# Branch hints ahead of the last branches of SyncE, VectorE and TensorE, with SyncE's end in a block of its own

## Chip, cores, metric

One Trainium2 chip, one core of it. The metric is the device time of one execution in microseconds (us); a time quoted for a kernel is the median of its runs on the chip.

## The reference

One decoding step for 8 sequences: attention of one query against a cache of 4096 keys and values in 32 heads of 128, beside a GELU MLP, added up.

```python
def _A_ref(x, k_cache, v_cache, wq, wo):        # B, H, Sk, Dh = 8, 32, 4096, 128
    q = (x @ wq).reshape(B, 1, H, Dh) ...
    p = softmax(einsum("bhqd,bhkd->bhqk", q, k_cache) * Dh ** -0.5)
    return einsum("bhqk,bhkd->bhqd", p, v_cache) ... @ wo
def _B_ref(x, w1, b1, w2, b2):
    return gelu(layernorm(x) @ w1 + b1) @ w2 + b2
xn = layernorm(x)
return x + _A_ref(xn, ...) + _B_ref(xn, ...)
```

Keys and values are 2 x 268 MB in bf16. Everything else is small beside them.

## The kernel before

SyncE issues all large loads in order: wq, w1, then K and V in 32 tiles (equal parts), then w2 and wo. Each load has 128 rows, in the trace 128 packets; a K or V load lands 19.35 us after the one before it and one of its 64 KB packets takes 2.42 us, so each of the 16 DMA engines has 8 of them. SyncE's queue keeps the 16 engines busy for 99.7% of the span. VectorE multiplies K by the query, TensorE sums and then weights V; a last block of PE multiplies by w2 and wo. In the profile VectorE is DVE, TensorE is PE (its weight loads PEld), ScalarE is ACT, and SPq is SyncE's sequencer, which issues loads. PE's program is 783 instructions long: a prologue, a loop over tiles, and the last block written out.

```python
    # SyncE: the K and V loads, then the last weights, then the end
    for t in range(1, NT):
        sy.wait_ge(sem["kf"], NX * (t - 1) + 2)
        load_kv(k_v, t, 0)
        sy.wait_ge(sem["vf"], t)
        load_kv(v_v, t, 1)
    # [cut: w2]
    for n, (r0, r1) in enumerate(zip(CUTS, CUTS[1:])):      # wo in four pieces
        if n == 1:
            sy.wait_ge(sem["kf"], NX * (NT - 1) + 5)
        wo_in.append(nc.alloc_semaphore(f"in_wo{n}"))
        sy.dma_start(out=wo_rows(r0, r1), in_=wo_v[:, r0 * D:r1 * D]).then_inc(wo_in[-1], 16)
    # [cut]
    sy.wait_ge(fin_d, 1)
    sy.dma_start(out=out2[:, :ND], in_=fin[:B]).then_inc(sem["out"], 16)
    sy.sem_inc(sent)
    sy.wait_ge(sem["out"], 32).then_inc(sem["out"], -32)

    # VectorE and ScalarE: a loop of 16 turns of two tiles, then the end
    with nc.Fori(0, NT // 2, 1, engines=[ENG.DVE, ENG.Activation]) as it:
        for u in range(2):
            vector_tile(2 * it + u, u)
            scalar_tile(u)
    # [cut]
    ve.wait_ge(sem["end"], 2)
    ve.tensor_copy(out=fin[:B], in_=acc[0][:B, :ND]).then_inc(fin_d, 1)

    # TensorE: blocks "head", "tile", "product", "values", "project"
    te.br_lt(regs["turns"], NT, on_true="tile", on_false="project")
    block("project")
    # [cut: 72 matmuls on w2, 8 on the heads]
    for n, (r0, r1) in enumerate(zip(CUTS, CUTS[1:])):
        te.wait_ge(wo_in[n], 16)
        rows = wo_rows(r0, r1).rearrange("p (r d) -> p r d", d=D)
        for r in range(r0, r1):
            ins = accumulate(te, OT[:, r, :], rows[:, r - r0, :], stop=(r == RO - 1))
    ins.then_inc(sem["end"], 1)
```

The softmax here doesn't subtract the row's maximum and nothing guards it: scores larger than these inputs give would overflow.

## Time and profile before

| | before |
|---|---|
| median of the first 3 runs | 1292.96 us |
| span of the profiled run | 1291.5 us |
| mean DMA rate | 431 GB/s |
| fetches of code in the span | 3 of 16 KB, 1 of 8 KB |

The page of the kernel before, its head, the DMA row of the 40 slices (busy tenths), and its table of DMA queues (packets, MB, share of the 16 engines):

```profile
span 1291.5 us, 14658 instructions
PE 736.8 (57%) x4707; PEld 322.3 (25%) x4707; DVE 829.4 (64%) x740; ACT 56.8 (4%) x181; POOL 2.4 (0%) x12
...
DMA  9999999999999999999999999999999999999998
...
q1 hardware_dynamic: 10368, 556.93, 99.7%
q8 instruction: 3, 0.05, 0.0%
q10 hardware_dynamic: 38, 0.02, 0.0%
q14 instruction: 1, 0.01, 0.0%
```

No engine is near full, the DMA is. The packets of the two queues of kind "instruction" are told here as the engines' code fetches: by their sizes 16 KB each on q8 (16,384 bytes), 8 KB each on q14 (8,192 bytes). That the large ones are TensorE's and the small ones VectorE's or SyncE's is read from their times.

The chain that ended last, in order of time (start, length, what):

```profile
1259.36 0.33 SPq L481
1259.69 0.05 issue
1259.74 28.52 DMA ring<-in_A_wo_dram
1288.26 0.04 issue
1288.31 1.29 PE acc L374 x18
1289.60 0.02 issue
1289.62 0.45 DVE fin L604
```

The end hangs on the landing of the third piece of wo at 1288.26 us. What comes after it takes 3.2 us.

The trace has 16 records of the load's semaphore, the counter that PE waits on, for each load, one for each DMA engine; PE's next matmul starts 0.05 us after the sixteenth (1288.31 after 1288.26 us). For that piece of wo, these are the times of the 16 records, against the last one:

```
before, third piece of wo (last at 1288.26 us):
-1.88 -1.88 -1.87 -1.80 -1.74 -1.63 -1.62 -1.58 -1.53 -1.46 -1.42 -1.41 -1.38 | -0.20 -0.11 0.00
```

Thirteen engines are done 1.4 us before the end, three are late. The three late ones go back to the fetches. The DMA table of the kernel before for 28 to 33, 50 to 55, 74 to 79 and 1286 to 1290 us, in this order:

```profile
q1 hardware_dynamic: 32, 2.10, 97.3%
q8 instruction: 1, 0.02, 1.3%
...
q1 hardware_dynamic: 31, 2.03, 94.6%
q14 instruction: 1, 0.01, 0.4%
...
q1 hardware_dynamic: 31, 2.03, 94.4%
q8 instruction: 1, 0.02, 1.3%
...
q1 hardware_dynamic: 170, 0.44, 27.5%
q8 instruction: 1, 0.02, 1.7%
```

The packets of the trace give their times, and, followed engine by engine (a data packet starts 3 or 4 ns before its forerunner ends), what each does to its engine:

| start | size | took | the engine's next 64 KB data packet (elsewhere 2.42 us) | lateness left behind |
|---|---|---|---|---|
| 29.93 us | 16 KB | 1.018 us | 2.886 us | 1.49 us |
| 52.15 us | 8 KB | 0.309 us | 3.033 us | 0.92 us |
| 75.96 us | 16 KB | 1.048 us | 2.888 us | 1.52 us |

(The last column is the fetch and what the next packet took over 2.418 us.) A further 16 KB at 1287.07 us falls on an engine that has just delivered its last data, and 8 KB at 1291.59 us come after the last wait of SyncE. The landings of the first loads show when an engine falls behind: one late engine at 46 us, two at 66 us, three at 85 us, and three ever after.

### The profile page before, as it was taken

The numbers are of one execution on the slowest core, as the hardware profiler recorded it, in microseconds if no ns is written. First come the engines' busy times: TensorE is split into PE (matmuls) and PEld (weight loads), VectorE is DVE, ScalarE is ACT, GpSimd is POOL, SyncE is SP. The second block draws the span as 40 slices with busy tenths as digits, with TensorE's granted clock in tenths as the row PEclk, the third lists the DMA queues.
The fourth block names the chain that finished last, engine by engine and source line by source line (L and its number), as shares of the span: only waits on it lengthen the run. The fifth ranks groups of instructions, "written<-read, shape, count | busy, mean of one in ns | idle before, by whom it ended". The sixth has DMA issues, their size and how long they took to land. (4 is left out here: it accounts for less than half of the span.)

```text
span 1291.5 us, 14658 instructions
## 1 busy us (share of the span) xinstructions
PE 736.8 (57%) x4707; PEld 322.3 (25%) x4707; DVE 829.4 (64%) x740; ACT 56.8 (4%) x181; POOL 2.4 (0%) x12
## 2 busy tenths in 40 slices
PE   4654565554565554665554565554566554565557
PEld 1222232222222222222222232222222222222223
DVE  2655677655677655677655677655677655577654
ACT  2000000000000000000000000000000000000000
POOL 0000000000000000000000000000000000000000
PEclk8778887778887777887777887778887777888779
DMA  9999999999999999999999999999999999999998
GB/s 419 441 427 440 430 428 449 422 428 449 422 428 449 422 430 447 422 436 440 424 436 438 426 438 434 428 442 428 428 449 422 428 449 422 428 449 422 430 447 350
DMA packets 10410, 557.02 MB, mean 431 GB/s; under 512 B 1163, under 2 KB 1188, under 8 KB 1446
## 3 DMA queue, kind: packets, MB, share of 16 engines
q1 hardware_dynamic: 10368, 556.93, 99.7%
q8 instruction: 3, 0.05, 0.0%
q10 hardware_dynamic: 38, 0.02, 0.0%
q14 instruction: 1, 0.01, 0.0%
HBM read 556.94 MB, written 0.01 MB: 431 GB/s over the span
## 5 line engine op out<-in xcount | busy, mean ns | idle before, releaser
L643 PE MATMUL s_ps<-ring,ident 128*128 x2048 | 544.5, 423 | 514.1 <-PEq L641 513.1
L559 DVE TENSOR_TENSOR ring<-ring,qb 128x4096 bf16<-128x4096 bf16 x256 | 579.2, 2283 | 281.6 <-DMA ring<-in_A_k_cache_dram 281.3
L643 PEld LDWEIGHTS s_ps<-ring,ident 128*128 128x128 bf16 x2048 | 217.4, 106 | 828.3 <-issue 678.5
L534 DVE TENSOR_REDUCE sc<-s_ps 128x32 f32<-128x512 f32 x256 | 171.8, 684 | 0.0
L662 PE MATMUL o_ps<-ring,ebd 128*32 128x512 bf16 x2048 | 116.4, 380 | 0.0
L546 DVE TENSOR_TENSOR ebd<-es,head 128x1536 bf16<-128x1536 bf16 x64 | 77.9, 1218 | 0.0
L569 DVE RECIPROCAL rec<-tot_ps 128x8 f32<-128x8 f32 x32 | 6.6, 208 | 110.7 <-PE oT_ps L670 110.7
L582 ACT ACTIVATE es<-sc 128x192 bf16<-128x192 f32 x64 | 19.8, 310 | 1104.2 <-DVE sc L534 1104.2
L662 PEld LDWEIGHTS o_ps<-ring,ebd 128*32 128x32 bf16 x2048 | 51.6, 97 | 62.5 <-issue 13.6
L670 PE MATMUL oT_ps<-selc,ob 128*128 128x8 f32 x256 | 33.9, 259 | 12.3 <-ACT ob L586 12.3
L670 PEld LDWEIGHTS oT_ps<-selc,ob 128*128 128x128 f32 x256 | 31.0, 191 | 15.2 <-ACT ob L586 15.2
L586 ACT ACTIVATE ob<-o_ps 128x512 f32<-128x512 f32 x32 | 19.1, 597 | 80.2 <-PE o_ps L662 80.2
L425 DVE TENSOR_SCALAR ring<-ring 96x384 f32<-96x384 f32 x2 | 0.7, 352 | 26.4 <-ACT ring L424 26.4
L545 DVE TENSOR_TENSOR Es<-Ep 128x1 f32<-128x1 f32 x32 | 5.1, 160 | 13.3 <-ACT es L582 13.3
L666 PEld LDWEIGHTS tot_ps<-headf,Es 128*128 128x128 f32 x64 | 9.5, 187 | 13.6 <-issue 13.6
L666 PE MATMUL tot_ps<-headf,Es 128*128 128x8 f32 x64 | 12.4, 266 | 0.0
L582 ACT ACTIVATION_READ_ACCUMULATOR es<-sc 128x1 f32 x64 | 11.9, 186 | 0.0
L414 PE MATMUL o_ps<-ring 128*32 128x384 bf16 x27 | 7.8, 860 | 2.8 <-DMA ring<-in_B_w_dram 2.8
L574 DVE TENSOR_TENSOR Ox<-on,quad 128x32 bf16 x32 | 6.2, 192 | 4.8
L414 PE MATMUL s_ps<-ring 128*32 128x384 bf16 x27 | 7.9, 862 | 0.0
L374 PE MATMUL acc<-ring,hT_sb 128*8 128x288 bf16 x72 | 6.0, 335 | 2.8 <-DMA ring<-in_B_w_dram 2.8
L336 PE MATMUL tot_ps<-ident,ring 40*128 40x16 bf16 x9 | 0.7, 204 | 11.8 <-DVE ring L314 11.8
(76 smaller groups left out, 61.2 us busy)
## 6 DMA issues: line engine op xcount, KB each, us to landing
ring<-in_B_w_dram SPq DMA_DIRECT2D x2, 5184.0 KB, 25.2
ring<-in_A_wq_dram SPq DMA_DIRECT2D x1, 4608.0 KB, 13.7
ring<-in_A_wo_dram SPq DMA_DIRECT2D x1, 1728.0 KB, 28.6
ring<-in_A_wo_dram SPq DMA_DIRECT2D x1, 1584.0 KB, 26.5
ring<-in_A_wo_dram SPq DMA_DIRECT2D x1, 1008.0 KB, 28.5
ring<-in_A_k_cache_dram SPq DMA_DIRECT2D x32, 31.9
ring<-in_A_v_cache_dram SPq DMA_DIRECT2D x32, 30.5
ring<-in_A_wo_dram SPq DMA_DIRECT2D x1, 288.0 KB, 28.8
```

Source lines behind the costliest of these rows:

```text
L414: i = e.matmul(h_ps[j][s * MP:(s + 1) * MP], lhsT=lhsT, rhs=wv[:, r0:r0 + HK, :], **flags)
L534: ins = ve.tensor_reduce(out=sc[:, n * CB:(n + 1) * CB], in_=bank_of(x).rearrange("p (c d) -> p c d", d=DL), axis=AX.X, op=ALU.add)
L546: ve.tensor_tensor(out=ebd[:, ja:jb], in0=es[:, a:b].rearrange("p (j c) -> p j c", c=4).unsqueeze(2) .to_broadcast([P, nj, G, 4]), in1=hea ...
L559: ve.tensor_tensor(out=k, in0=k, in1=qb[:, bass.ds(t, 1), :].to_broadcast([P, CB, Dh]), op=ALU.mult,).then_inc(sem["prod"], 1)
L569: ve.reciprocal(out=rec[:], in_=tot_ps[:, :G]).then_inc(sem["rec"], 1)
L574: ve.tensor_tensor(out=Ox[:, bass.ds(t, 1)].rearrange("p o g m -> p (o g) m"), in0=on[:].unsqueeze(2).to_broadcast([P, G, M]), in1=quad[:] ...
L582: sa.activation(out=es[:, a * CB:b * CB], in_=sc[:, a * CB:b * CB], func=ACT.Exp, scale=scale, accum_out=Ep[:, i:i + 1]).then_inc(sem["x"], 1)
L586: sa.activation(out=ob[:].rearrange("r c d -> r (c d)"), in_=o_ps, func=ACT.Copy).then_inc(sem["ob"], 1)
L643: ins = te.matmul(to, lhsT=idn, rhs=k[:, :, d * DL:(d + 1) * DL], start=(d == 0), stop=(d == Dh // DL - 1))
L662: ins = te.matmul(o_ps[m * MP:(m + 1) * MP, :], lhsT=ebd[:, j].rearrange("p g c -> p (g c)"), rhs=vals[:, c:c + 4, :], start=(j < M), stop ...
L666: te.matmul(tot_ps[:, :G], lhsT=Es[:].to_broadcast([P, P]), rhs=headf[:], start=True, stop=True).then_inc(sem["vf"], 1)
L670: ins = te.matmul(oT_ps[:, :G], lhsT=ob[:, c, :], rhs=selc[:, c, :], start=(c == 0), stop=(c == 3))
```

## The change

Its intent: to be rid of the fetches at 52.15, 1287.07 and 1291.59 us, which I took to bring code that their engine does not run; the trace does not show what a fetch brings. In the program a hint names the last branch and its target ahead of time; that the fetch is then not made was my hope. A hint is put on a branch, so SyncE's last four instructions go into a block of their own, and VectorE and TensorE get an empty last block.

```diff
+    vector_last = nc.mark_branch_hint_location(ENG.DVE)      # at the start of the program
+    sync_last = nc.mark_branch_hint_location(ENG.SP)
@@ SyncE, after the last piece of wo is issued
+    sy.br("sync_end").branch_hint(sync_last)
@@
-    sy.wait_ge(fin_d, 1)
-    sy.dma_start(out=out2[:, :ND], in_=fin[:B]).then_inc(sem["out"], 16)
-    sy.sem_inc(sent)
-    sy.wait_ge(sem["out"], 32).then_inc(sem["out"], -32)
@@ after the last work of VectorE
+    ve.br("vector_end").branch_hint(vector_last)
+    block("vector_end", ENG.DVE)
+
+    block("sync_end", ENG.SP)
+    sy.wait_ge(fin_d, 1)
+    sy.dma_start(out=out2[:, :ND], in_=fin[:B]).then_inc(sem["out"], 16)
+    sy.sem_inc(sent)
+    sy.wait_ge(sem["out"], 32).then_inc(sem["out"], -32)
@@ TensorE
     block("project")
+    place = nc.mark_branch_hint_location(ENG.PE)
@@
     ins.then_inc(sem["end"], 1)
+    te.br("tensor_end").branch_hint(place)
+    block("tensor_end")
```

More of the change, by code (lines that the diff above doesn't have):

```diff
@@ L480, in decode @@
         wo_in.append(nc.alloc_semaphore(f"in_wo{n}"))
-        sy.dma_start(out=wo_rows(r0, r1), in_=wo_v[:, r0 * D:r1 * D]).then_inc(wo_in[-1], 16)
+        to, rows = wo_rows(r0, r1), wo_v[:, r0 * D:r1 * D]
+        sy.dma_start(out=to, in_=rows).then_inc(wo_in[-1], 16)
+    sy.br("sync_end").branch_hint(sync_last)
     BLOCKS = [(7, 0, 1, 2, 3, 4, 5, 6), (0, 7, 1, 2, 3, 4, 5, 6)]
```

## The prediction

> **What bounds the kernel.** The DMA stream. The page's slices show the 16 DMA engines 90% or more busy in 39 of 40 slices, 431 GB/s over 1291.5 us; VectorE is busy 64%, PE 57%. The chain that ended last runs through an output-weight load (issued 1259.74, landed 1288.26 us), then 18 PE matmuls (1.29 us), a VectorE copy (0.45 us) and the output DMA (issued 1290.09, landed 1291.48). Only the landing of the last weights and the 3.2 us after it count.
>
> **Code fetches in the trace.** The DMA table lists 16 KB fetches on one queue (3) and 8 KB fetches on another. Packets by time:
> - 29.9 us, 16 KB, 1.02 us: PE in its prologue.
> - 52.2 us, 8 KB, 0.31 us: [...]I give it to VectorE.
> - 76.0 us, 16 KB, 1.05 us: PE turns from first to second tile.
> - 1287.1 us, 16 KB, 1.09 us: PE in its last block.
> - 1291.59 us, 8 KB: 70 ns after SyncE's last wait; I give it to SyncE.
>
> [...]
>
> The first three sit on three different DMA engines of a saturated stream. There the data stop for the fetch, and the next packet takes longer too (2.89 or 3.03 us, not 2.42). Sum: about 1.47 us for a PE fetch, 0.92 us for VectorE's. That lag is never made up: from 85 us on, every K and V load has three late landings, 0.18, 0.11 and 0.00 us before the last; the other 13 are 1.35 us or more ahead. So it still is at the weights that end the chain.
>
> **What the change does.** It adds three hints and three taken branches; the program order shows that nothing else moves. SyncE's hint precedes the issue of the first K load (which queues behind 26 us of data), VectorE's a wait for x (5.5 us), PE's a wait for w2 (1277.9 us); the branches follow the last work or fall in SyncE's 29 us wait. Direct cost on the chain: none.
> If hints work as meant, the fetches at 52.2, 1287.1 and 1291.6 us vanish. But:
> - PE's fetches at 30 and 76 us stay: [...]PE's hint runs only near 1276 us. By the landings, the last of the three late engines is the one with the 76 us fetch, VectorE's the earliest. Removing that moves the last landing by 0.
> - The 1287.1 us fetch is on an engine that has just finished its data, and ends at 1288.15, before the landing that matters.
> - The last is after the last wait: at most about 0.1 us.
>
> So: three fetches fewer and almost no time, 1292.75 us against 1292.96, range 1291.9 to 1293.4. Faster by over 2%: 0.3%; within 2%: 99.4%; slower: 0.3%.
>
> **What would show it.** DMA table: 16 KB fetches 3 to 2, 8 KB fetches 1 to 0 in the span. Landings: two late engines, not three, the last as far behind as before. Chain of waits: same pieces, last weights landing near 1288.2 us. Busy times unchanged.
>
> **What would make it wrong.** PE's two early fetches change too (gain up to 1.3 us). [...] Or SyncE's new block starts a fresh code block, fetched near 1260 us, on the stream's tail.

Four passages are cut, at the marks: a source for the order of fetches; a reason for giving the 52 us fetch to VectorE (in the trace PE works at that time too, its product matmuls from 49.42 us on); a reason why PE's two early fetches stay; and a guess at what a hint might do. The fetches removed were put at 0, 0 and at most 0.1 us (an estimate from the 70 ns), and the forecast was 1292.75 us, 0.21 us less than the 1292.96 us measured before it.

## The result, and the profile after

| | before | after |
|---|---|---|
| median | 1292.82 us (6 runs, 1292.57 to 1293.12) | 1292.91 us (6 runs, 1292.73 to 1293.85) |
| span of the profiled run | 1291.5 us | 1291.5 us |
| 16 KB fetches | 29.93, 75.96, 1287.07 us | 29.99, 75.88 us |
| 8 KB fetches | 52.15, (1291.59) us | 1264.16 us |
| late engines at the third piece of wo | three | two |
| its landing | 1288.26 us | 1288.17 us |

The ratio is 1.0002, 95% interval 0.9989 to 1.0015. A ratio is the mean time of one kernel's fast runs over that of the other's in the same rounds, so not quite the ratio of the medians quoted. The time is the same.

The page after, the head and the queues:

```profile
span 1291.5 us, 14664 instructions
PE 734.5 (57%) x4707; PEld 321.8 (25%) x4707; DVE 829.2 (64%) x740; ACT 56.7 (4%) x181; POOL 2.4 (0%) x12
...
q1 hardware_dynamic: 10368, 556.93, 99.7%
q8 instruction: 2, 0.03, 0.0%
q10 hardware_dynamic: 38, 0.02, 0.0%
q14 instruction: 1, 0.01, 0.0%
```

One 16 KB fetch is gone. The count of 8 KB fetches in the span is one as before, but it is another one. The DMA table after, for 28 to 33, 50 to 55, 74 to 79 and 1260 to 1268 us:

```profile
q1 hardware_dynamic: 31, 2.03, 94.3%
q8 instruction: 1, 0.02, 1.3%
...
q1 hardware_dynamic: 32, 2.10, 96.9%
...
q1 hardware_dynamic: 31, 2.03, 94.4%
q8 instruction: 1, 0.02, 1.3%
...
q1 hardware_dynamic: 131, 3.19, 93.1%
q14 instruction: 1, 0.01, 0.2%
```

In the second stretch there is no instruction line any more: the fetch at 52 us is gone. In the fourth there is one that the kernel before does not have there. It starts 3.5 us after SyncE's new branch (1260.61 us) and makes a third engine somewhat late, beside the two of TensorE's fetches:

```
after, third piece of wo (last at 1288.17 us):
-1.84 -1.83 -1.69 -1.63 -1.61 -1.53 -1.43 -1.43 -1.42 -1.37 -1.34 -1.20 -1.13 -0.87 | -0.03 0.00
```

The chain that ended last, after:

```profile
1252.92 24.91 DMA ring<-in_B_w_dram
1277.83 0.04 issue
1277.87 4.49 PE acc L377 x36
1282.36 0.54 PE s_ps L701 x8
1282.90 6.68 PE acc L377 x100
1289.58 0.03 issue
1289.60 0.45 DVE fin L604
```

It starts from the landing of w2 instead of wo, and PE then has no pause to the end. The reason is not the change but the clock of that execution. The stretches view for 1277.5 to 1290 us, first the kernel before, then after (columns: stretch, its length, busy us of PE, PEld, DVE, ACT, POOL, granted TensorE clock, DMA share, GB/s):

```profile
1277.50:1290.00 12.50, 10.57 (x144) 6.58 (x144) 0.81 (x2) 0.38 (x1) 0.00 (x0) 0.87 0.77 321
```

```profile
1277.50:1290.00 12.50, 11.69 (x144) 7.13 (x144) 0.82 (x2) 0.40 (x1) 0.00 (x0) 0.75 0.76 319
```

The same 144 matmuls ran at a granted clock of 0.75 instead of 0.87. A second profile of the changed kernel (below, after_again) has 0.86 there and the chain through wo, as before; of the other runs, sync_only too has 0.75 there and the chain from w2. PE ended at the same time in both (1289.60 us before, 1289.58 us after), so at 0.75 PE only just keeps up with the landings.

### The profile page after: what moved, and what is told of

The parts are those of the page before. It is cut to its first block, busy times and chain, and to the rows that moved or that the text cites. A ratio compares the mean times of both kernels' runs of the same rounds, so it can differ in the third digit from the quotient of the medians.

```text
span 1291.5 us, 14664 instructions
## 1 busy us (share of the span) xinstructions
PE 734.5 (57%) x4707; PEld 321.8 (25%) x4707; DVE 829.2 (64%) x740; ACT 56.7 (4%) x181; POOL 2.4 (0%) x12
```

## The experiments

Theory: the end of the stream is set by the DMA engine that carried the most code fetches. TensorE's two fetches at 30 and 76 us, which stay, put one on each of two engines; the removed ones were on others, or after their engine's data. Rivals: lateness of one engine does not matter; or each fetch costs its bytes; or the hints did not do what took the fetches away. "no_sync" is the change without SyncE's part, and the base of the kernels with longer PE code and of the last experiment.

### The change once more

No edit.

> The changed kernel unchanged, five more rounds, for its spread and to see whether its fetches come at the same times. Theory (SyncE's new block moves SyncE's fetch from after the end to about 1264 us, into the tail of the stream, on an engine that differs from run to run): the profile shows an 8 KB fetch between 1260 and 1268 us again; median 1292.9 us, and about one execution in six is 0.5 to 1 us longer, because the fetch falls on one of the two engines that are already late. Rival (the two long executions, 1293.3 and 1293.9 us, are chance of the chip): before shows such executions as often in these rounds.

Measured: 1292.97 us (5 runs, 1292.71 to 1293.00), before 1292.94 us in the same rounds, ratio 1.0000. The 8 KB fetch is there again, at 1264.85 us. There was no long execution in five; of the eleven of the changed kernel two were over 1293.2 us, and the kernel before has shown one of 1293.37 us in other rounds. So the risk that I saw in SyncE's moved fetch was not shown: the two long executions may be chance. A 16 KB fetch of PE also appeared here at 1290.28 us, 1.2 us after PE's last branch; the first profile of the change has none. It falls after the stream. Of the twelve profiles of kernels with TensorE's part, six have such a fetch, about 1 to 4 us after PE's last branch, and six have none. So with TensorE's part that fetch was not in the stream (1287.07 us before, 1286.99 us in sync_only), but it did not always go.

### Without SyncE's part

```diff
-    sync_last = nc.mark_branch_hint_location(ENG.SP)
-    sy.br("sync_end").branch_hint(sync_last)
     [and SyncE's last four instructions back in their old place]
```

> Only the hints of VectorE and TensorE; SyncE as before. Theory: 16 KB fetches at 30 and 76 us alone, no 8 KB fetch inside the span, the 8 KB fetch just after SyncE's last wait is back (1291.6 us); two late engines; median 1292.8 us within 0.2 us of before, and no execution above 1293.2 us. Rival (the hint of VectorE did not take away the 52 us fetch, but something of SyncE's did): the 52 us fetch is back.

Measured: 1292.90 us (5 runs, 1292.79 to 1293.07), ratio 1.0000. The fetches are at 29.74 and 76.02 us and, of 8 KB, at 1291.71 us alone. Two late engines: the third piece of wo has fourteen at 1.51 us or more before the last, then -0.40 and 0.00. So VectorE's part took the 52 us fetch away (TensorE's hint runs only at 1275 us), and this moved the last landing nowhere (1288.35 us; 1288.17 and 1288.35 us in the two profiles of the change, 1288.26 us before). Whether it was VectorE's hint, or the branch and the empty block that came with it, was not tried apart.

### SyncE's part alone

```diff
     [of the change, the lines of VectorE and TensorE left out]
```

> Only SyncE's part of the change (block and hint). Theory: 16 KB fetches at 30, 76 and 1287 us and VectorE's 8 KB at 52 us stay, SyncE's 8 KB moves from after the end to near 1264 us; three late engines as before, and a fourth one 0.3 to 0.5 us late of the other twelve from the loads of 1278 us on; 1292.9 us within 0.3. Rival (SyncE's part is what took the 52 us fetch away): it is missing here.

Measured: 1292.95 us (4 runs, 1292.80 to 1293.12), ratio 1.0000. Fetches at 29.94, 52.14, 76.00, 1264.39 and 1286.99 us. Landings of the third piece of wo: twelve engines to -1.22, one at -0.73, three at -0.20, -0.13 and 0.00 us. The theory's picture, line by line; the rival about the 52 us fetch falls. The 1287 us fetch, back without TensorE's hint, costs nothing.

### What moved SyncE's fetch to 1264 us

"Boundary" in the expectations stands for the point of SyncE's program at which an 8 KB fetch comes; it is known only by the time of that fetch in the runs, 1264.78 us in sync_plain and 910.43 us in sync_pad_plain. Cut at the marks are guesses at where SyncE's instructions lie and at how a hint works, which no trace here shows.

```diff
-    sy.br("sync_end").branch_hint(sync_last)
+    sy.br("sync_end")        # dropped in compilation: the block comes next
```

> The changed kernel with SyncE's end still in its own block, but no hint on SyncE (the compiler then drops the branch, since the block comes next). Theory [...]: the 8 KB fetch 3 to 5 us after SyncE's last weight load (1263 to 1266 us) is there without the hint. Rival (the hint, or the taken branch, fetches): no 8 KB fetch near 1264 us; it comes after SyncE's last wait, near 1291.6 us, as before the change. Time 1292.9 us within 0.3 either way.

Measured: 1293.17 us (4 runs, 1292.82 to 1293.38), ratio 1.0002. The 8 KB fetch is there at 1264.78 us, without a hint or a branch. So it comes with the block, not the hint.

```diff
     load_kv(k_v, 0, 0)
+    filler = nc.alloc_semaphore("filler")
+    for _ in range(24):
+        nc.sync.sem_inc(filler)
     [the rest of the change as it is]
```

> The whole change, with 24 cheap semaphore increments ahead in SyncE's program, so that SyncE passes its block boundary in the middle of its loads (near 900 to 1000 us) rather than at its end. Theory 1 [...]: nothing near 900 to 1000 us, a fetch of 8 KB 3 to 5 us after the branch at 1260.6 us as in the changed kernel. Theory 2 [...]: no fetch of SyncE at all, the hint suppresses the one at the boundary. Theory 3 (the hint of SyncE does nothing): 8 KB at 900 to 1000 us and none near 1264 us. The time is 1292.9 us within 0.3 in all of them.

Measured: 1292.84 us (4 runs, 1292.67 to 1293.00), ratio 0.9998. No 8 KB fetch from the start of the span on: what theory 2 expected.

```diff
     [sync_pad without SyncE's hint]
-    sy.br("sync_end").branch_hint(sync_last)
+    sy.br("sync_end")
```

> sync_pad without SyncE's hint. Theory (the hint is what kept SyncE's block boundary in the middle of its loads from fetching): an 8 KB fetch appears between 850 and 1000 us, and a third engine is late from then on by about 0.9 us more than its fellows. Rival (SyncE passes no boundary there at all): no 8 KB fetch in the span, as in sync_pad. Time 1292.9 us within 0.4 either way.

Measured: 1292.71 us (one run, state unknown). An 8 KB fetch at 910.43 us. The DMA table of this kernel for 905 to 915 us, and after it that of sync_pad for the same stretch:

```profile
q1 hardware_dynamic: 72, 4.46, 103.3%
q14 instruction: 1, 0.01, 0.2%
```

```profile
q1 hardware_dynamic: 68, 4.33, 99.9%
```

The hint is one of two differences; the other is the branch itself, which goes with it, but which sync_pad reaches only at 1260.76 us. So with the hint, run 1.3 us after the start in sync_pad, the fetch at 910 us is not made. This rests on one profile of each kernel. One engine fell behind at that fetch: in the K load that lands at 897.7 us the third-last engine is 0.84 us before the last, in that of 936.4 us 0.59 us, from a place among those at about 1.3 us. That is 0.74 us, and the packets say 0.72; I had expected 0.9. Why the block of its own brought the fetch forward, from 1291.6 to 1264 us, is not shown: the trace does not tell where instructions lie.

### More fetches on TensorE

The tiles' loop is written out, in full or for the first tiles, which lengthens PE's program and adds fetches of 16 KB (37 before the landing of the third piece of wo with 9,810 instructions, two in no_sync with 785); arithmetic and waits stay.

```diff
+    for turn in range(32):                     # or 16, 8, 6, 4, with the loop kept after it
+        for x in range(NX):
+            te.wait_ge(sem["prod"], 1).then_inc(sem["prod"], -1)
+            for d in range(Dh // DL):
+                ins = te.matmul(to, lhsT=idn, rhs=k[:, :, d * DL:(d + 1) * DL], ...)
+        [the code of "values", as in the loop]
-    block("tile") ... te.br_lt(regs["turns"], NT, on_true="tile", on_false="project")
```

> As no_sync, but TensorE's loop over 32 tiles is written out straight, 9,810 instructions instead of 785, so that TensorE fetches some 37 blocks of 16 KB during the stream instead of 2. Its arithmetic and its waits stay. Theory (each fetch makes its DMA engine about 1.47 us late for good, and the last engine sets the end): 37 fetches over 16 engines are 2 or 3 on each if dealt evenly, so the last engine is 3 x 1.47 = 4.4 us late where it was 1.47: about 1295.8 us, 2.9 us more; if engines are drawn at random, the worst has 5 or 6, up to 1300 us. The landings of one load spread over several steps. Rival A (lateness of an engine is absorbed by the others): 1292.8 us within 0.3. Rival B (only the bytes count): 0.6 MB more at 431 GB/s, 1.4 us more.

Measured: 1299.13 us (5 runs, 1298.97 to 1299.41), before 1292.94 us, ratio 1.0049 (interval 1.0035 to 1.0062): 6.19 us more. Both rivals fall: A by 6 us, B by 4.8 us. My number was off too, by 3.3 us, and the landings tell why. The page's queues of this kernel, and its chain:

```profile
q1 hardware_dynamic: 10368, 556.93, 99.4%
q8 instruction: 38, 0.62, 0.2%
```

```profile
1265.73 28.61 DMA ring<-in_A_wo_dram
1294.33 0.04 issue
1294.38 1.29 PE acc L375 x18
```

The chain is that of before, 6.07 us later from the landing of wo on (1294.33 against 1288.26 us). Landings of the third piece of wo:

```
unroll32 (last at 1294.33 us):
-6.39 -6.27 -6.18 -6.16 -6.10 -6.10 -6.03 -5.79 | -1.57 -1.48 -1.47 | -0.24 -0.23 -0.10 -0.03 0.00
```

Eight engines have no fetch of PE at all. 37 fetches lie before this landing; dealt in turn over the other eight they are five on five of them and four on three: exactly the groups. I had counted on 16 engines.

The same trace shows the delay build up step by step. A K or V load has its last landing 19.35 us after the one before it (19.2 to 19.5 us from 65 us on), except at four places, each after the first fetch of a new round of eight:

| fetch, by count | starts at | last landing of the next load | after the landing before it |
|---|---|---|---|
| 9th | 307.14 us | 318.87 us | 20.79 us |
| 17th | 608.66 us | 610.87 us | 20.99 us |
| 25th | 890.79 us | 902.51 us | 20.83 us |
| 33rd | 1163.21 us | 1174.94 us | 20.83 us |

The other fetches of these rounds move no last landing by more than 0.1 us. The four steps add up to 6.0 us; the end is 6.07 us later. unroll16 (below) shows the first two of them, 20.78 and 20.89 us.

One more thing differs from the kernel before: the eight engines without a fetch paused here. The first of them had delivered the load of 902.51 us at 895.87 us; SyncE had issued the V load that follows only at 895.28 us, and the first landing of that V load came 20.5 us after the first of the load before it instead of 19.35. Their lead shrinks by this: at the end the first engine is done at 1287.94 us, not at 1286.38 as before, and the groups are closer together than the counts of fetches would put them. The last engine, which sets the end, kept to its 19.35 us there.

"By the count" in the next four expectations is my estimate of the fetches from the length of PE's program; what the runs show for it is 35 more fetches in unroll32 for 9,025 more instructions, one for each 258. Cut from that of unroll6 are a figure used in the count, and the groups of four and four engines, where the landings of unroll32 above have five and three.

> As unroll6 with 4 tiles written out, so that no fetch falls into the end of the stream: 6 fetches of 16 KB by the count (7 if the block count is one off), all on different engines. In unroll6 eight fetches had left the last landing of each load where two leave it, and a ninth, unexpected one at 1281.6 us cost 1.5 us. Theory (the largest number of fetches on one engine sets the end): 1292.9 us within 0.3, six or seven late engines, all within 0.5 us of one another. Rival (each further fetch costs its share, 0.18 us): 1293.6 us or more.

> As no_sync, with the first 6 tiles of TensorE written out and the loop kept for the other 26: [...]8 fetches of 16 KB within the stream in place of 2. The run with all tiles written out showed eight engines without a fetch[...]. Theory (TensorE's fetches are dealt in turn over eight of the 16 engines, and the engine with the most of them sets the end): 8 fetches put one on each of the eight, none has two, so the time is that of before, 1292.9 us within 0.3, with eight late engines in the landings. Rival (each further fetch costs its share, 6.2 us for 35 more, 0.18 us each): 6 more cost 1.1 us, 1294.0 us.

> As unroll6, with 8 tiles written out: 11 fetches by the count. Theory of the turn over eight engines: three of the eight have two fetches, so the last engine is one fetch later than before, 1.47 us: 1294.4 us within 0.3; landings in three steps of about 1.45 us (eight, five, three engines). Rival of a share for each: 9 more cost 1.6 us, 1294.5 us; it is told apart by unroll6 and unroll16, and by the landings.

> As unroll6, with 16 tiles written out: 20 fetches by the count, two or three on each of eight engines. Theory: two fetches more than now on the last engine, 2.9 us: 1295.8 us within 0.3; landings: eight engines early, four late by two fetches, four by three. Rival of a share for each: 18 more cost 3.2 us, 1296.1 us.

| kernel | fetches before that landing | engines with 0, 1, 2 ... fetches, as the landings group | most on one | time, us | against before, same rounds |
|---|---|---|---|---|---|
| no_sync | 2 | 14, 2 | 1 | 1292.90 | -0.04 |
| unroll4 | 6 | 10, 6 | 1 | 1293.23 | +0.22 |
| unroll6 | 9 | 8, 7, 1 | 2 | 1294.73 | +1.72 |
| unroll8 | 11 | 8, 5, 3 | 2 | 1294.73 | +1.72 |
| unroll16 | 20 | 8, 0, 4, 4 | 3 | 1296.01 | +3.00 |
| unroll32 | 37 | 8, 0, 0, 0, 3, 5 | 5 | 1299.13 | +6.19 |

The time follows the largest number on one engine, and not the number of fetches. From unroll4 on, a step costs 1.5 us (one to two), 1.3 us (two to three) and 1.6 us each (three to five): six cost next to nothing, and nine cost as much as eleven. The ranges of runs of the steps do not overlap (unroll4 ends at 1293.34 us, unroll6 begins at 1294.23). In unroll6 my count was wrong by one fetch. At 1281.61 us, 6.5 us after TensorE's hint, a ninth came, and one of the eight engines had its second. Up to then the landings were as expected: the V load that landed at 1265.65 us has eight late engines, and 2.02 us between first and last, as no_sync has with two (2.03 us). So it is a missed number and a good witness: that one fetch, so near the end, cost 1.5 us of landing. The hint did not hold it back, for a reason that was not tried; a tenth fetch came at 1294.43 us, after the branch. In unroll4 most of the 0.2 us over before is in the landing of the third piece of wo: 1288.41 us, against 1288.26 before.

### Fetching early

TensorE is idle until 11.8 us. Can its two early fetches be had for nothing there?

```diff
-    te.br("head")
+    te.br("touch")
-    te.br_lt(regs["turns"], NT, on_true="tile", on_false="project")
+    te.br_lt(regs["turns"], NT, on_true="tile", on_false="leave")
+    block("leave")
+    te.wait_ge(w2_in, 16)
+    te.br("project")
+    block("touch")
+    te.wait_ge(od.sem("gpsimd"), 1)
+    te.br("head")
     block("project")
     [cut]
-    te.wait_ge(w2_in, 16)      # this wait now stands in "leave"
```

> As no_sync, but TensorE, idle until 11.8 us, first branches to a stub that lies in the code block fetched at 30 us before, and back, so that its two blocks are fetched in the first 5 us. Theory: the lateness depends on a fetch sharing an engine with a stream that never pauses, not on when: two 16 KB fetches between 1 and 5 us, none at 30 and 76 us, two late engines through the whole run, 1292.8 us within 0.3. Rival (while the stream starts the engines have room): no late engine, last landing 1.1 to 1.3 us earlier, 1291.6 us.

Measured: 1293.50 us (5 runs, 1292.73 to 1294.77), ratio 1.0004. The fetches are at 6.06 and 11.58 us, later than I expected, and none at 30 and 76 us. Two late engines all the same (-0.12 and 0.00 us, the next at -1.12), the third piece of wo at 1288.22 us. So fetches at 6.06 and 11.58 us left the last landing where those at 30 and 76 us leave it (1288.26 us before); the rival falls. The greater spread has more than one source. In the profiled run the span is 1291.5 us but the time 1293.66, and a 16 KB fetch of PE starts at 1292.95 us, after the last instruction. One other execution has a span of 1293.4 us, which I can't explain without its trace.

## Why the prediction was right

- **The end hangs on the late engines of the stream.** Shown: six kernels that differ in PE's fetches end in steps of 1.3 to 1.6 us by the largest number of fetches on one engine, and within unroll32 the landings slip by 1.4 to 1.6 us at the first fetch of each new round and at no other.
- **The fetches at 52 us and 1287 us go.** Right for the stream; TensorE's came after its last branch in six of twelve profiles. The 52 us fetch was VectorE's, as said: it is gone without SyncE's part and there with SyncE's part alone.
- **PE's fetches at 30 and 76 us stay, and removing the others moves the last landing by 0.** Right: two late engines instead of three, and landings of the third piece of wo within 0.1 us of before.
- **The 1287 us fetch lies after its engine's data.** Right in the two traces that have it: with it and without it, the landing and the time are the same.
- **The fetch after the end goes too, at most 0.1 us.** Half right. It left the end, but SyncE's new block brought it to 1264 us. The prediction had named that as a way to be wrong, with a fetch "near 1260 us, on the stream's tail". It cost nothing in the profiled runs: in the profile after, one of the engines about 1.6 us ahead fell back to 0.87 us, and such a lateness of 0.7 us fits into the lead. That it fell on an engine with a lead in all four profiles that have it is luck as far as the prediction goes; on an engine already late it would have cost some 0.7 us (an estimate from the 0.72 us that the packets of this fetch show). The prediction's words of a fresh code block are not shown, only the time of the fetch.
- **8 KB fetches 1 to 0 in the span, and the same pieces in the chain.** Wrong in both: one for the reason above, and the chain of the first profile after, because that execution had a granted clock of 0.75 in PE's last block.
- **Sizes.** A PE fetch was put at 1.47 us of lateness. By the packets it is 1.48 to 1.58 us (1.43 us in touch, among smaller packets). The 8 KB fetch was put at 0.92 us; it was 0.92 to 0.93 us where VectorE made it at 52 us, 0.72 to 0.73 us where SyncE made it (at 910 us in one run, near 1264 us in four).

PE's fetches follow the length of its program: unroll32 has 9,810 instructions and 37 fetches before the end of its stream, unroll16 has 5,393 and 20, so 17 more for 4,417 more, one for each 260.

None of the runs beats the kernel before. The theory says what would: no fetch of PE at all during the stream, worth an estimated 1.1 to 1.4 us (the distance from the thirteenth engine to the last in the landings above). I found no form of PE's program (783 instructions) without its two early fetches in the stream and tried none but touch, where they still fell into it.

## What to carry to other kernels

When a kernel is bound by a DMA stream that never pauses, look at the landings of one load engine by engine: each code fetch seen here, of TensorE, VectorE or SyncE, that fell into the stream's data made one DMA engine late (1.43 to 1.58 us for 16 KB, 0.72 to 0.93 us for 8 KB) for as long as the stream did not pause, and only the latest engine counted. Removing one of several fetches bought nothing while another engine was as late (1292.91 against 1292.82 us); adding four cost 0.2 us (unroll4), but with two on the same engine it was 1.7 us (unroll6). Before hinting the last branch, find which fetches stay anyway (here those at 30 and 76 us), and look where a block of its own moves the next fetch (here SyncE's, from 1291.6 to 1264 us).
